# Re-laying a serial chain, its load queue and a job mixture in a fused attention and feed-forward backward kernel

## The chip, the cores and the metric

One core of one Trainium2 chip. The metric is the device time of one execution in microseconds (us). The kernel before takes 1837.25 us (median of 16 executions, 1830 to 1842).

## The reference, cut to what matters

The function is one decode step of a block with adaptive layernorm, and its backward pass: attention over a key and value cache of 2 x 32 heads x 8192 keys x 128, then a gated feed-forward layer. All gradients are outputs, those of both caches too.

```python
h = _layernorm(x) * (1 + ca) + sa
q = (h @ wq).reshape(B, 1, 32, 128).transpose(0, 2, 1, 3)
p = softmax(einsum('bhqd,bhkd->bhqk', q, k_cache) * 128 ** -0.5)
o = einsum('bhqk,bhkd->bhqd', p, v_cache)
x = x + ga * (o.reshape(B, 1, 4096) @ wo)
h = _layernorm(x) * (1 + cb) + sb
x = x + gb * ((silu(h @ w1) * (h @ w3)) @ w2)
# outputs: x, and the vjp for x, k_cache, v_cache, wq, wo, w1, w3, w2, c, w_mod
```

The caches are read (K once, V twice, because dV and dK need V again after the whole forward and feed-forward pass of that batch) and their gradients written. That is nearly all of the 718 MB that the kernel moves.

## The kernel before

The kernel is written as a static schedule. Work is put into numbered *slots*, and the slots are then emitted in order. A slot is a place in each engine's program, not a time. There are three kinds of work.

- An **A job** (64 of them, one for each batch and head, eight slots each): load K and V of the head, transpose K on TensorE, scores, exp, weighted sums of V and K.
- A **C job** (64, eight slots each): load V again, compute dV and dK on VectorE as outer products, store them. It needs dO of its head, so it can start only after its batch's chain.
- A **chain** for each batch: everything serial between that batch's last A job and its first C job, that is wo, layernorm, the feed-forward layer, its gradients and finally dO for all heads.

```python
def lay(steps, slot):                  # each step is (slots to advance, function)
    for n, f in steps:
        at(slot, PL_TASK, f)
        slot += n
    return slot

sA = [NG * i for i in range(H)]        # NG = 8: A jobs of batch 0
CS0 = end_a(sA[H - 1]) + 1             # 272: chain of batch 0 starts
TC = CS0 + length(ch[0]) + 1           # 330: chain (57 slots) is over
...
while len(sA) < NHD:                   # after TC, C and A jobs alternate
    if s >= TC and len(sC) < H and (not sC or sC[-1] < s - NG):
        sC.append(s)
    else:
        sA.append(s)
    s += NG
...
at(TC, PL_TASK, ffn_done)              # gives back two big buffers (w1, w3, w2)
```

The first C job comes at slot 336. Until then A jobs fill the slots, so the chain's instructions stand between theirs. The last part of the chain is dO: sixteen groups, each eight transposes of wo, one copy out of PSUM on VectorE, eight matmuls with one column, one group to a slot.

```python
def turned_steps(put, groups, done):
    ...
        nc.tensor.transpose(tp[:r, j, :], src, identb[:])
        kt = ktp.tile([P, GRP, P], BF16, name="kt", tag="kt")
        nc.vector.tensor_copy(kt[:r, 0:len(blocks), :], tp[:r, 0:len(blocks), :])
    ...
turned_steps(put, ogroups, lambda k, ps: nc.vector.tensor_copy(DO32[:, b, 2 * k:2 * k + 2], ps))
```

Loads are issued by one queue, in order of need. There are five *big* buffers (2 MB) and eleven *half* buffers (1 MB); V takes a big one, or two halves. The weights of the chain need big ones: two for wo, loaded once for both batches, and two for w1, w3 and w2, loaded again for batch 1.

```python
def pump():
    while loads:
        _, _, kind, f = loads[0]
        ...
        if kind == "big" and free["big"] < 1:
            return                     # nothing behind it is loaded either
        ...
        loads.pop(0)
        f()
```

## Time and profile before

| stretch of the span, us | what runs | GB/s | TensorE busy |
|---|---|---|---|
| 0 to 413 | A alone | 375 | 367 of 413 us |
| 413 to 497 | A and the chain of batch 0 | 293 | 74 of 84 us |
| 497 to 557 | A and dO of batch 0 | 285 | 55 of 60 us |
| 557 to 1128 | A and C in turn | 416 | 78% |
| 1128 to 1306 | C and the chain of batch 1 | 387 | 70% |
| 1306 to 1790 | C, small weight gradients | 416 | 71% |

The page shows the span in forty slices; each digit is a busy share in tenths, and the last line the rate of all DMA in each slice.

```profile
span 1835.9 us, 60759 instructions
...
PE   6988999898998777777778876677867777767561
...
DMA  9998998988679999999999999999999999999997
GB/s 386 421 411 323 377 399 327 418 316 332 252 288 373 425 417 421 420 423 419 417 421 407 416 423 393 414 356 377 422 408 412 412 416 424 418 423 402 427 418 292
```

From the thirteenth slice on the DMA engines are nearly always fully busy, at about 416 GB/s. There TensorE has room. In the slices just before, TensorE is at nine tenths and the rate falls to 252. So the kernel has two kinds of stretch, and time is to be had only where the rate is below 416. The windows view puts numbers on the stretches. Its columns are the window, its length, busy us of each engine with the count of instructions, the granted TensorE clock, the DMA engines' busy share, and GB/s.

```profile
core 0: us, PE busy (x) PEld busy (x) DVE busy (x) ACT busy (x) POOL busy (x), PEclk, DMA share, GB/s
0.00:413.00 413.00, 366.73 (x8603) 360.28 (x8604) 230.38 (x374) 225.70 (x305) 102.31 (x166) 0.99 0.95 375
413.00:497.00 84.00, 74.00 (x1693) 72.72 (x1690) 45.90 (x106) 34.98 (x49) 10.04 (x25) 0.88 0.77 293
497.00:557.00 60.00, 55.42 (x1283) 54.17 (x1280) 40.39 (x81) 26.93 (x39) 7.06 (x19) 0.97 0.76 285
557.00:1128.00 571.00, 444.49 (x8820) 430.69 (x8818) 386.51 (x456) 293.36 (x409) 99.15 (x205) 0.81 1.01 416
1128.00:1306.00 178.00, 125.42 (x2208) 116.98 (x2206) 135.82 (x223) 78.61 (x115) 21.93 (x41) 0.67 0.97 387
```

The view of waits, for the load queue on SyncE between 250 and 425 us, shows what held the loads (columns: who waited, for what, us in total, times, longest). L155 and L163 load K and V; L525 and L513 are loads of w1/w3 and of wo.

```profile
SPq L155 <- PE m_ps L455: 49.0, 12, 5.9
SPq L163 <- PE m_ps L455: 41.1, 8, 5.9
SPq L525 <- PE m_ps L455: 18.7, 2, 9.6
SPq L513 <- PE m_ps L455: 15.3, 2, 10.2
```

For 34 us the queue stood with a weight load at its head that waited for a big buffer. The Trainium skill ("DMA: Bandwidth & Descriptors", section "Anatomy of one DMA — SWDGE (gpsimd) path") says that a semaphore wait happens on the issuing sequencer before dispatch, not in the DMA engines. That section describes loads issued by GpSimd; these are issued by SyncE. The trace agrees: the wait stands on SyncE's sequencer, and no K or V load is issued behind it (none from 291.5 to 312 us, where the two buffers for w1, w3 and w2 are waited for).

### The profile page before, as it was taken

The numbers are of one execution on the slowest core, as the hardware profiler recorded it, in microseconds if no ns is written. First come the engines' busy times: TensorE is split into PE (matmuls) and PEld (weight loads), VectorE is DVE, ScalarE is ACT, GpSimd is POOL, SyncE is SP. The second block draws the span as 40 slices with busy tenths as digits, with TensorE's granted clock in tenths as the row PEclk, the third lists the DMA queues.
The fourth block names the chain that finished last, engine by engine and source line by source line (L and its number), as shares of the span: only waits on it lengthen the run. The fifth ranks groups of instructions, "written<-read, shape, count | busy, mean of one in ns | idle before, by whom it ended". The sixth has DMA issues, their size and how long they took to land. (4 is left out here: it accounts for less than half of the span.)

```text
span 1835.9 us, 60759 instructions
## 1 busy us (share of the span) xinstructions
PE 1416.7 (77%) x27206; PEld 1316.5 (72%) x27206; DVE 1177.8 (64%) x1602; ACT 953.9 (52%) x1359; POOL 330.8 (18%) x621
## 2 busy tenths in 40 slices
PE   6988999898998777777778876677867777767561
PEld 5988999898998777777778776676645555646561
DVE  2555556674666666667666667688845565656694
ACT  3555666554445455544555544434755565757451
POOL 0222222231012111111111111111111211111111
PEclk9999999998999788887887787577655555857675
DMA  9998998988679999999999999999999999999997
GB/s 386 421 411 323 377 399 327 418 316 332 252 288 373 425 417 421 420 423 419 417 421 407 416 423 393 414 356 377 422 408 412 412 416 424 418 423 402 427 418 292
DMA packets 99425, 718.11 MB, mean 391 GB/s; under 512 B 10160, under 2 KB 17020, under 8 KB 26332
## 3 DMA queue, kind: packets, MB, share of 16 engines
q1 hardware_dynamic: 57936, 430.00, 58.3%
q0 software_dynamic: 41216, 284.22, 37.3%
q8 instruction: 213, 3.49, 0.7%
q14 instruction: 48, 0.39, 0.1%
q10 hardware_dynamic: 12, 0.01, 0.0%
HBM read 429.99 MB, written 284.20 MB: 389 GB/s over the span
## 5 line engine op out<-in xcount | busy, mean ns | idle before, releaser
L395 ACT COPY kt<-tp 128x1024 bf16<-128x1024 bf16 x768 | 774.1, 1015 | 645.0 <-PE tp L390 636.9
L390 PE MATMUL tp<-identb,half 128*128 128x128 bf16 x5248 | 467.4, 241 | 38.9 <-issue 16.9
L455 PE MATMUL m_ps<-e,half 128*128 128x1 bf16 x4096 | 405.4, 170 | 3.1 <-issue 3.0
L390 PEld LDWEIGHTS <-half 128*128 128x128 bf16 x5248 | 355.4, 108 | 66.8 <-issue 43.4
L992 DVE TENSOR_TENSOR half<-DOr,e 128x2048 bf16<-128x2048 bf16 x256 | 311.8, 1218 | 131.4 <-DMA out_dram<-half 131.2
L992 DVE TENSOR_TENSOR half<-Qr,ds 128x2048 bf16<-128x2048 bf16 x256 | 310.2, 1220 | 78.7 <-DMA out_dram<-half 77.3
L455 PEld LDWEIGHTS <-half 128*128 128x128 bf16 x4096 | 353.3, 97 | 4.1 <-issue 3.9
L393 DVE COPY kt<-tp 128x1024 bf16<-128x1024 bf16 x256 | 176.2, 688 | 262.5 <-PE tp L390 251.7
L390 PE MATMUL tp<-identb,big 128*128 128x128 bf16 x2944 | 305.8, 267 | 13.3 <-DMA big<-in_A_v_cache_dram 12.3
L438 DVE TENSOR_TENSOR ek<-half,e 128x2048 bf16<-128x2048 bf16 x256 | 307.9, 1219 | 3.1 <-ACT e L430 2.2
L997 POOL DMA_DIRECT2D out_dram<-half x256 | 136.3, 532 | 954.0 <-DVE half L992 672.7
L390 PEld LDWEIGHTS <-big 128*128 128x128 bf16 x2944 | 230.8, 120 | 102.6 <-issue 88.8
L453 PE MATMUL m_ps<-ek,half 128*128 128x129 bf16 x2240 | 247.5, 228 | 55.8 <-DVE ek L438 54.8
L453 PEld LDWEIGHTS <-half 128*128 128x128 bf16 x2240 | 210.9, 106 | 60.0 <-issue 58.9
L969 PEld LDWEIGHTS <-kt 128*128 128x128 bf16 x4096 | 187.4, 108 | 80.6 <-DVE kt L393 51.7
L969 PE MATMUL s_ps<-DO_bf,kt 128*128 128x1 bf16 x4096 | 192.7, 168 | 67.9 <-DVE kt L393 47.1
L440 POOL COPY ek<-e 128x16 bf16<-128x16 bf16 x256 | 133.0, 540 | 431.8 <-ACT e L430 225.8
L411 PE MATMUL s_ps<-qT_bf,kt 128*128 128x1 bf16 x4096 | 178.5, 164 | 20.9 <-issue 9.5
L453 PE MATMUL m_ps<-ek,big 128*128 128x129 bf16 x1856 | 186.2, 218 | 3.9 <-issue 3.9
L411 PEld LDWEIGHTS <-kt 128*128 128x128 bf16 x4096 | 159.3, 97 | 26.2 <-issue 12.9
L453 PEld LDWEIGHTS <-big 128*128 128x128 bf16 x1856 | 156.9, 96 | 3.2 <-issue 3.0
L1113 ACT CAST stg<-m_ps 128x512 bf16<-128x512 f32 (+2 forms) x123 | 71.9, 594 | 113.4 <-DMA out_dram<-stg 96.2
(221 smaller groups left out, 805.4 us busy)
## 6 DMA issues: line engine op xcount, KB each, us to landing
out_dram<-half POOLq DMA_DIRECT2D x256, 1024.0 KB, 16.5
big<-in_A_v_cache_dram SPq DMA_DIRECT2D x75, 2048.0 KB, 17.3
half<-in_A_k_cache_dram SPq DMA_DIRECT2D x128, 1024.0 KB, 13.0
half<-in_A_v_cache_dram SPq DMA_DIRECT2D x106, 1024.0 KB, 21.1
out_dram<-stg POOLq DMA_DIRECT2D x22, 512.0 KB, 20.8
big<-in_B_w_dram SPq DMA_DIRECT2D x4, 1376.0 KB, 13.7
big<-in_A_wq_dram SPq DMA_DIRECT2D x8, 512.0 KB, 13.0
big<-in_A_wo_dram SPq DMA_DIRECT2D x2, 2048.0 KB, 9.5
```

The lines of the kernel that those rows point to most:

```text
L390: nc.tensor.transpose(tp[:, j, :], block(j), identb[:])
L393: nc.vector.tensor_copy(kt[:], tp[:])
L395: nc.scalar.copy(kt[:], tp[:])
L411: nc.tensor.matmul(S_ps[i][:, cc:cc + 1], kt[:, j, :], qT_bf[:, h, b:b + 1], start=True, stop=True)
L438: nc.vector.tensor_tensor(pair(t[:, :, 0:P]), pair(K[(i, hf)][:, o:o + QK, :]), E2[i][:, ks, :].unsqueeze(2).to_broadcast((P, QK, P // 2, ...
L440: nc.gpsimd.tensor_copy(t[:, :, P:P + 1], E2[i][:, ks, 0:1])
L453: nc.tensor.matmul(m[:, 0:P + 1], vb_(V[i], kk), t[:, kk % QK, 0:P + 1], start=(kk == 0), stop=(kk == KK - 1), skip_group_check=True)
L455: nc.tensor.matmul(m[:, P + 1:P + 2], kb_(K, i, kk), E2[i][:, kk, 0:1], start=False, stop=(kk == KK - 1), skip_group_check=True)
L969: nc.tensor.matmul(DP[n][:, cc:cc + 1], kt[:, j, :], DO_bf[:, b, h:h + 1], start=True, stop=True)
L992: nc.vector.tensor_tensor(pair(t[:, o:o + QK, :]), QD[(n, which)][:].rearrange("p (a b) -> p a b", b=2).unsqueeze(1).to_broadcast((P, QK, ...
L997: sq_.dma_start(src_of(dst, n)[:, hf * HK:(hf + 1) * HK, :], t[:])
L1113: nc.scalar.copy(st["t"][:lw, o:o + rw], ps[:lw, 0:rw])
```

## The change

The intent is to shorten the time in which TensorE works through A jobs and the chain together, and to start the C jobs, and with them the full DMA rate, earlier. It has five parts:

1. The chain is packed into 23 slots, several steps to a slot, and its dO part is taken out as separate steps. Batch 0's dO steps are strewn through the mixture of A and C, each just before the C jobs that need it.
2. The first C job comes at slot 304 instead of 336; A and C then alternate with 25 C jobs instead of 22.
3. The two feed-forward buffers are given back at slot 295 instead of 330.
4. A load that lacks a big buffer may be passed by the loads behind it (until slot 292).
5. dO's copies out of PSUM go from VectorE to ScalarE, and the layernorms' Sqrt and reciprocal become Ln and Exp.

```diff
-        nc.scalar.activation(std[:], s2[:], ACT.Sqrt, bias=eps_t[:], scale=1.0 / D)
-        nc.vector.reciprocal(rstd_t[:], std[:])
+        nc.scalar.activation(std[:], s2[:], ACT.Ln, bias=eps_t[:], scale=1.0 / D)
+        nc.scalar.activation(rstd_t[:], std[:], ACT.Exp, scale=-0.5)
 ...
     def pump():
-        while loads:
-            _, _, kind, f = loads[0]
+        j = 0
+        while j < len(loads):
+            _, _, kind, f = loads[j]
 ...
             if kind == "big" and free["big"] < 1:
-                return
+                if now[0] > CS0 + 20:
+                    return
+                j += 1
+                continue
 ...
-            loads.pop(0)
+            loads.pop(j)
 ...
+    def steps_do(b, k):                          # dO of two heads: tr, mm, sig
+        def tr():
+            ... eight transposes of wo into tp ...
+            nc.scalar.copy(kt[:], tp[:])
+        def mm():
+            ... eight matmuls with d_attn ...
+            nc.vector.tensor_copy(DO_bf[:, b, hs], ps)
+            nc.vector.tensor_mul(DOr_bf[:, b, hs], ps, rtot[:, b, hs])
+            ...
+        return [(1, tr), (1, mm), (1, sig)]
 ...
-        put(1, tot)
+        put(0, tot)                              # and so on for the other steps
 ...
-    TC = CS0 + length(ch[0]) + 1
+    E0 = CS0 + length(ch[0])
+    TC = E0 + 5
 ...
+    for k in range(H // 2):
+        lay(steps_do(0, k), E0 if k == 0 else max(E0 + 3 * k, sC[2 * k] - 10))
     t1 = lay(ch[1], CS1)
-    s = max(s, t1 + 4)
+    s = max(s, t1 + 5)
+    for k in range(H // 2):
+        lay(steps_do(1, k), t1)
+        t1 += 2
 ...
-    at(TC, PL_TASK, ffn_done)
+    at(E0, PL_TASK, ffn_done)
```

(The new loop that places the mixture, the changes of the other chain steps, and the removal of the old dO code are cut.)

More of the change, by code (lines that the diff above doesn't have):

```diff
@@ L544 @@
     O_bf = hcol("O_bf", BF16)
-    DO32 = hcol("DO32")
     DO_bf = hcol("DO_bf", BF16)
@@ L646, in tr, with sig @@
             st[("t", k)] = kt
-        def mm(k):
-            st[("p", k)] = groups[k][1](st.pop(("t", k)))
         def step(k):
-            if 0 <= k - 2 < len(groups):
-                done(k - 2, st.pop(("p", k - 2)))
             if k < len(groups):
                 tr(k)
-            if 0 <= k - 1 < len(groups):
-                mm(k - 1)
-        for k in range(len(groups) + 2):
+            if k > 0:
+                done(k - 1, groups[k - 1][1](st.pop(("t", k - 1))))
+        for k in range(len(groups) + 1):
             put(1, lambda k=k: step(k))
+    def steps_do(b, k):
+        out = []
+        st = {}
+        hs = slice(2 * k, 2 * k + 2)
+        def tr():
+            tp = tps.tile([P, GRP, P], BF16, name="tp", tag="tp")
+            for n in range(2):
+                for dc in range(NC):
+                    h = 2 * k + n
+                    nc.tensor.transpose(tp[:, n * NC + dc, :],
+                                        wo_v[h // (H // 2)][:, h % (H // 2), dc * P:(dc + 1) * P], identb[:])
+            kt = ktp.tile([P, GRP, P], BF16, name="kt", tag="kt")
+            nc.scalar.copy(kt[:], tp[:])
+            st["kt"] = kt
+        def mm():
+            ps = scr(2)
+            kt = st.pop("kt")
+            for n in range(2):
+                for dc in range(NC):
+                    nc.tensor.matmul(ps[:, n:n + 1], kt[:, n * NC + dc, :], d_attn_bf[:, dc, b:b + 1],
+                                     start=(dc == 0), stop=(dc == NC - 1))
+            nc.vector.tensor_copy(DO_bf[:, b, hs], ps)
+            nc.vector.tensor_mul(DOr_bf[:, b, hs], ps, rtot[:, b, hs])
+            pr = tmp.tile([P, 2], F32, name="prod", tag="prod", bufs=2)
+            nc.vector.tensor_mul(pr[:], O32[:, b, hs], ps)
+            st["pr"] = pr
+        def sig():
+            ps = scr(2)
+            nc.tensor.matmul(ps, onesf[:], st.pop("pr")[:], start=True, stop=True)
+            nc.vector.tensor_copy(SIG[:, b, hs], ps)
+        return [(1, tr), (1, mm), (1, sig)]
     def steps_chain(b):
@@ L679, in otask @@
             nc.vector.tensor_copy(O_bf[:, b, :], O32[:, b, :])
-        put(1, tot)
+            nc.vector.scalar_tensor_tensor(Qr_bf[:, b, :], qT[:, :, b], SCL, rtot[:, b, :], ALU.mult, ALU.mult)
+        put(0, tot)
         put(1, otask)
@@ L691, in attn_ev @@
             nc.vector.tensor_copy(attn[:, dc, b:b + 1], hold[dc])
-        for dc in range(NC):
-            def f(dc=dc):
-                if dc > 0:
-                    attn_ev(dc - 1)
-                attn_pe(dc)
-            put(1, f)
-        put(1, lambda: attn_ev(NC - 1))
+        put(1, lambda: (attn_pe(0), attn_pe(1)))
+        put(0, lambda: (attn_pe(2), attn_pe(3)))
+        put(0, lambda: [attn_ev(dc) for dc in range(NC)])
         def x1_task():
@@ L721, in ln_a @@
             nc.vector.tensor_sub(v[:], st[:, 1:2], sq[:])
-            hold["v"] = v
             hold["st"] = st
-        def ln_s():
-            nc.scalar.activation(hold["v"][:], hold["v"][:], ACT.Sqrt, bias=eps_t[:])
+            nc.scalar.activation(v[:], v[:], ACT.Ln, bias=eps_t[:])
+            nc.scalar.activation(rstd2[:, 0, b:b + 1], v[:], ACT.Exp, scale=-0.5)
         def ln_b():
-            nc.vector.reciprocal(rstd2[:, 0, b:b + 1], hold["v"][:])
             nc.vector.tensor_scalar(xn2[:, :, b], x1[:, :, b], hold["st"][:, 0:1], rstd2[:, 0, b:b + 1],
@@ L737, in steps_chain @@
         put(1, x1_task)
-        put(1, sums)
+        put(0, sums)
         put(1, ln_a)
-        put(2, ln_s)
         put(1, ln_b)
@@ L754, in proj_ev, with p1, p2 @@
             nc.vector.tensor_copy(dst[:FL, FC - 1, b:b + 1], hold[nm][:FL, FC - 1:FC])
-        put(1, lambda: proj("w1"))
-        def p2():
+        def p1():
+            proj("w1")
             proj_ev("w1", gate)
-            proj("w3")
-        put(1, p2)
-        def p3():
             hold["e"] = small(FC, "sge", b)
             nc.scalar.activation(hold["e"][:], gate[:, :, b], ACT.Exp, scale=-1.0)
+        put(1, p1)
+        def p2():
+            proj("w3")
             proj_ev("w3", up)
-        put(1, p3)
+        put(0, p2)
         def p4():
@@ L791, in p5 @@
             nc.vector.tensor_add(dslg[:, :, b], e[:], hold["sig"][:])
-        put(1, p5)
+        put(0, p5)
         def p6():
@@ L841, in q3 @@
             nc.vector.tensor_mul(d_attn_bf[:, :, b], mod[:, 2 * NC:3 * NC, b], d_x1[:, :, b])
-        put(1, q1)
-        put(1, sums)
+        put(0, q1)
+        put(1, lambda: None)
+        put(0, sums)
         put(1, q3)
-        ogroups = []
-        for h0 in range(0, H, 2):
-            def blocks(h0=h0):
-                return [wo_v[h // (H // 2)][:, h % (H // 2), dc * P:(dc + 1) * P]
-                        for h in (h0, h0 + 1) for dc in range(NC)]
-            def mm(kt):
-                ps = scr(2)
-                for n in range(2):
-                    for dc in range(NC):
-                        nc.tensor.matmul(ps[:, n:n + 1], kt[:, n * NC + dc, :], d_attn_bf[:, dc, b:b + 1],
-                                         start=(dc == 0), stop=(dc == NC - 1))
-                return ps
-            ogroups.append((blocks, mm))
-        turned_steps(put, ogroups, lambda k, ps: nc.vector.tensor_copy(DO32[:, b, 2 * k:2 * k + 2], ps))
-        def z1():
-            nc.vector.tensor_copy(DO_bf[:, b, :], DO32[:, b, :])
-            nc.vector.tensor_mul(DOr_bf[:, b, :], DO32[:, b, :], rtot[:, b, :])
-            nc.vector.scalar_tensor_tensor(Qr_bf[:, b, :], qT[:, :, b], SCL, rtot[:, b, :], ALU.mult, ALU.mult)
-            pr = small(H, "prod", b)
-            nc.vector.tensor_mul(pr[:], O32[:, b, :], DO32[:, b, :])
-            hold["pr"] = pr
-        def z2():
-            hold["sg"] = scr(H)
-            nc.tensor.matmul(hold["sg"], onesf[:], hold["pr"][:], start=True, stop=True)
-        put(1, z1)
-        put(1, z2)
-        put(1, lambda: nc.vector.tensor_copy(SIG[:, b, :], hold["sg"]))
         return out
@@ L900 @@
     s = NG * H
-    while len(sA) < NHD:
-        if s >= TC and len(sC) < H and (not sC or sC[-1] < s - NG):
+    while len(sA) < NHD and s < TC:
+        sA.append(s)
+        s += NG
+    na, ncc = NHD - len(sA), max(0, H - 1 - -(-(length(ch[1]) + 5 + MOFF) // NG))
+    for k in range(na + ncc):
+        if len(sC) * (na + ncc) <= k * ncc and len(sC) < ncc:
             sC.append(s)
@@ L913 @@
     lay(ch[0], CS0)
+    for k in range(H // 2):
+        lay(steps_do(0, k), E0 if k == 0 else max(E0 + 3 * k, sC[2 * k] - 10))
     t1 = lay(ch[1], CS1)
-    s = max(s, t1 + 4)
+    s = max(s, t1 + 5)
+    for k in range(H // 2):
+        lay(steps_do(1, k), t1)
+        t1 += 2
+    t1 += 1
     sC += [s + NG * n for n in range(H)]
```

## The prediction

> **What bounds the kernel now.** Bytes: the page shows 718 MB in 1836 us, 391 GB/s on average; stretches with fully busy DMA engines move about 416. By stretches: 0 to 413 us (phase A alone: transposed K, scores, exp, weighted sums) 375 GB/s, TensorE busy 367 us, near its limit; 413 to 497 us 293 GB/s and 497 to 557 us 285 GB/s, TensorE busy 74 of 84 and 55 of 60 us: here batch 0's serial chain (wo, layernorm, feed-forward and its gradients, dO) is interleaved with phase A; 557 to 1128 us, A and C (dV, dK) jobs alternating, 416 GB/s, TensorE 78% busy: DMA-bound; 1128 to 1306 us, batch 1's chain among C jobs, 387; C alone to 1790 us, 416; the tail 291. Time is to be had only where the rate is below 416.
>
> **What the change does.** It shortens the chain from 57 slots to 23 plus sixteen dO steps laid separately. Batch 0's dO steps are strewn, just in time, through the A/C mixture instead of preceding it; the first C job comes at slot 304 instead of 336, the mixture holds 25 C jobs instead of 22. No byte and hardly a matmul is removed. dO's sixteen 128x1024 copies per batch go from VectorE (0.69 us each) to ScalarE (1.01 us): 11 us of VectorE time per chain. Two feed-forward buffers come free 35 slots earlier. The load queue may pass a load that lacks a big buffer. Sqrt plus reciprocal become Ln and Exp: the trace has seven table loads of 1283 ns (the Trainium skill, "ScalarE: Activation LUTs", "What ACT_TABLE_LOAD costs", states the same number); at most a few us, mostly hidden.
>
> **What it is worth.**
> 1. Slots 272 to 304 hold the same TensorE work before and after (four A jobs, about 430 chain matmuls at 42 to 50 ns), so 413 to 497 us hardly moves. Fewer slots between dependent steps may cost TensorE 2 to 6 us; an earlier V load may give 4 us back.
> 2. The 60 us at 285 GB/s go into the DMA-bound mixture; dO's 256 matmuls (11 us) hide in 22% idle TensorE. Of 718 MB, 539 are still to move at 497 us: 1295 us at 416 GB/s, plus 14 us lost in the tail and 4 to 8 us in chain 1: about 1811. This step gains 60 x (1 - 285/416) = 19 us.
> 3. Chain 1: 178 us at 387 GB/s lose 12 us against 416. With 11 us less VectorE work (VectorE was 76% busy) half comes back: 6 us.
> 4. Prefetch and tables: 0 to 5 us.
> Sum about 28 us off 1837.
>
> **Predicted: 1808 us**, range 1788 to 1830. Chances: faster by over 2% 0.33, within 2% 0.63, slower 0.04.
>
> **What would show each step right.** 416 GB/s should be reached near 500 us instead of 560 to 600; the stretch before should look unchanged. The chain-1 stretch should run near 400 GB/s. Bytes, matmuls and the last slice should be the same; VectorE's busy time about 20 us lower, ScalarE's 30 us higher. Table loads should be fewer than seven.
>
> **What would make it wrong.** If the early mixture does not reach 416 GB/s, because the first C jobs' V loads come too late or buffers run short, step 2 shrinks. If the denser chain makes TensorE wait for VectorE and ScalarE, step 1 becomes a loss. If chain 1's stretch was limited by the weights' reload and held buffers rather than VectorE, step 3 is nothing; if VectorE was all of it, the gain doubles and 2% is passed. If the early feed-forward buffers lift the rate before 500 us too, it is faster still.

## The result, and the profile after

The changed kernel takes 1808.36 us (median of eight, 1803.63 to 1811.9). The ratio to the kernel before is 0.9842, with a 95% interval of 0.9826 to 0.9858: a gain of 1.6%, clear of noise but less than 2%.

The page after, same lines as above:

```profile
span 1801.9 us, 60973 instructions
...
PE   6888999999888887877877788788778684866761
...
DMA  9998999997899999999999999999999999999997
GB/s 385 421 422 346 388 385 388 361 376 282 324 384 422 410 421 420 413 416 414 419 414 409 417 415 419 400 412 386 402 417 415 413 412 426 419 422 418 410 423 294
```

The windows view of the changed kernel:

```profile
0.00:413.00 413.00, 368.63 (x8717) 362.62 (x8718) 233.58 (x376) 228.64 (x311) 101.93 (x170) 1.00 0.97 386
413.00:497.00 84.00, 75.08 (x1763) 73.17 (x1761) 52.84 (x123) 38.00 (x55) 12.61 (x28) 0.92 0.76 294
497.00:557.00 60.00, 50.81 (x1125) 48.58 (x1124) 42.13 (x55) 35.68 (x50) 13.54 (x24) 0.94 1.00 399
557.00:1128.00 571.00, 458.35 (x8925) 444.19 (x8923) 385.02 (x495) 301.61 (x417) 90.67 (x199) 0.80 1.01 416
1128.00:1306.00 178.00, 140.72 (x2411) 132.88 (x2409) 132.96 (x263) 97.54 (x136) 25.23 (x45) 0.68 1.00 400
```

The stretch from 413 to 497 us is as it was (294 GB/s against 293). From 497 to 557 us the rate is 399 instead of 285, and TensorE has room there. Two gains stand elsewhere: 386 instead of 375 GB/s before 413 us, and 400 instead of 387 in batch 1's chain. The mixture's rate did not change; it is the same 416.

The waits of the load queue, 250 to 425 us, in the changed kernel (L529 and L517 are the weights):

```profile
SPq L155 <- PE m_ps L459: 56.3, 13, 7.1
SPq L163 <- PE m_ps L459: 43.0, 8, 6.6
...
SPq L529 <- PE m_ps L459: 10.7, 2, 5.8
SPq L517 <- PE m_ps L459: 10.4, 2, 5.3
```

The weights now hold the queue for 21 us instead of 34. The queue doesn't wait less in all: with every row of the view added up it is 149 us, against 146 before. What changed is which loads stand behind a wait.

A rate in a fixed window mixes a gain with a shift. Since both kernels move the same 718 MB, a better measure is the time at which the first N megabytes had been started. I worked it out from the DMA packets' start times and sizes in the traces of one execution each:

```
first N MB    before    after    lead
    100        259.1    254.6     4.5
    160        424.9    414.3    10.6
    200        567.4    538.1    29.3
    440       1143.0   1114.9    28.1
    540       1395.2   1361.5    33.6
    700       1778.4   1745.1    33.3
```

The lead is made in three places: about 10 us before the chain of batch 0 has done anything (160 MB; the 4.5 us at 100 MB are within what two executions can differ by, see below), about 19 us between 160 and 200 MB, where the old kernel worked through dO, and about 5 us between 440 and 540 MB, where batch 1's chain lies. Elsewhere the two run alike. Traces of two executions can differ by several us without a reason: kernels that start with the same program as the kernel before differ from it by up to 3 us at 100 MB and 4.7 us at 80 MB. The profiled execution of the changed kernel was also its fastest (1803.63 us), so the 34 us between the two profiled spans stand for 29 in the medians.

### The profile page after: what moved, and what is told of

Same layout as the page of the kernel before. It is cut to its first block, busy times and chain, and to the rows that moved or that the text cites. A ratio compares the mean times of both kernels' runs of the same rounds, so it can differ in the third digit from the quotient of the medians.

```text
span 1801.9 us, 60973 instructions
## 1 busy us (share of the span) xinstructions
PE 1428.4 (79%) x27266; PEld 1326.8 (74%) x27266; DVE 1164.3 (65%) x1655; ACT 983.4 (55%) x1394; POOL 329.5 (18%) x621
## 5 line engine op out<-in xcount | busy, mean ns | idle before, releaser
L394 PEld LDWEIGHTS <-half 128*128 128x128 bf16 x5248 | 356.7, 108 | 48.5 <-issue 38.0
L459 PEld LDWEIGHTS <-half 128*128 128x128 bf16 x4096 | 352.7, 97 | 6.8 <-issue 6.6
L394 PEld LDWEIGHTS <-big 128*128 128x128 bf16 x2944 | 231.1, 120 | 111.7 <-issue 110.8
L457 PE MATMUL m_ps<-ek,half 128*128 128x129 bf16 x2112 | 234.7, 229 | 24.4 <-DVE ek L442 22.9
L457 PEld LDWEIGHTS <-half 128*128 128x128 bf16 x2112 | 200.0, 106 | 24.8 <-issue 24.6
L457 PE MATMUL m_ps<-ek,big 128*128 128x129 bf16 x1984 | 198.3, 217 | 3.4 <-issue 3.4
L444 POOL COPY ek<-e 128x16 bf16<-128x16 bf16 x256 | 125.7, 510 | 395.6 <-ACT e L434 189.7
L457 PEld LDWEIGHTS <-big 128*128 128x128 bf16 x1984 | 166.7, 96 | 2.0 <-issue 1.9
```

The source lines that it names most:

```text
L394: nc.tensor.transpose(tp[:, j, :], block(j), identb[:])
L444: nc.gpsimd.tensor_copy(t[:, :, P:P + 1], E2[i][:, ks, 0:1])
L457: nc.tensor.matmul(m[:, 0:P + 1], vb_(V[i], kk), t[:, kk % QK, 0:P + 1], start=(kk == 0), stop=(kk == KK - 1), skip_group_check=True)
L459: nc.tensor.matmul(m[:, P + 1:P + 2], kb_(K, i, kk), E2[i][:, kk, 0:1], start=False, stop=(kk == KK - 1), skip_group_check=True)
```

## The experiments

Theory P (the prediction): TensorE limits the stretch before the mixture and DMA limits the mixture, so what counts is that dO and four A jobs were moved from the one into the other. Rival S: the gain comes from what surrounds it, that is the shorter chain, earlier buffers, the load queue, or the other engine for the copies. The experiments ran in three batches, each on one chip with its own runs of the kernel before: first do_first, the two do_twice and do_copies_vector; then old_queue, sqrt_back, late_buffers and before_early_buffers; then the other four. The ratio to those runs is given for each. The changed kernel's own ratio (0.9842) comes from none of these batches, so a difference between two such ratios is certain to about 0.002 or 0.003 only, that is 4 to 5 us. Each batch holds one kernel that can't be told from the changed one: do_copies_vector (0.9839), sqrt_back (0.9861) and early_buffers_1 (0.9837). Against these the differences within a batch can be read too. Every kernel gave a correct result.

### do_first: the placement alone is undone

```diff
-    TC = E0 + 5
+    TC = E0 + 35
...
-        lay(steps_do(0, k), E0 if k == 0 else max(E0 + 3 * k, sC[2 * k] - 10))
+        lay(steps_do(0, k), E0 + 2 * k)
```

> The changed kernel with its short chain, its ScalarE copies and its early buffers, but batch 0's dO steps laid at two slots each before the mixture, and the first C job at slot 336 as in the kernel before (22 C jobs in the mixture's equal part). Theory P (placement: dO's matmuls and four A jobs were moved out of a TensorE-limited stretch into a DMA-bound one): most of the gain goes, about 1825 us (ratio to before 0.990 to 0.998). Rival S (the shorter chain, the freed buffers, the load queue or the move to ScalarE give the gain): stays at 1808 to 1813 us (ratio 0.984 to 0.987).

Measured: 1820.1 us, ratio 0.9911 (0.9898 to 0.9925). The placement is worth 0.9911 - 0.9842 = 0.0069 of 1837, 12.7 us (13 us against do_copies_vector of the same batch). The rest, 16 us, stays without it. So both theories hold a part. The windows view of this kernel shows the placement's part:

```profile
497.00:557.00 60.00, 58.42 (x1379) 57.79 (x1376) 39.65 (x84) 39.32 (x53) 12.98 (x24) 1.00 0.75 285
557.00:1128.00 571.00, 426.73 (x8525) 414.81 (x8522) 381.16 (x446) 289.21 (x404) 97.67 (x198) 0.80 1.00 416
```

TensorE is busy 58.4 of 60 us and the rate is 285 GB/s again, as before the change, although this kernel has the packed chain, the early buffers, the new queue and the copies on ScalarE. By the bytes moved, its lead over the kernel before is 13.3 us at 160 MB and 12.7 at 200, where the changed kernel goes from 10.6 to 29.3. So these four do not fill this stretch here while dO stands in it. (Early buffers alone, in the kernel before, do lift it in part; see before_early_buffers.)

### do_twice_before and do_twice_after: dO's TensorE work doubled

Every transpose and matmul of dO is done twice, with the same result. In the changed kernel:

```diff
-                for dc in range(NC):
+                for dc in [d for d in range(NC) for _ in range(2)]:
                     h = 2 * k + n
                     nc.tensor.transpose(...)
...
-            for n in range(2):
+            for n in (0, 0, 1, 1):
                 for dc in range(NC):
                     nc.tensor.matmul(...)
```

and the same doubling in the kernel before.

> The kernel before with every dO transpose and matmul done twice (256 matmuls more per batch, same result). Theory P: batch 0's 256 fall in a stretch where TensorE is the limit, about 42 ns each, so +8 to +14 us (1845 to 1851 us); batch 1's are mostly hidden. Rival (TensorE is not what holds that stretch, but buffers or waits): +0 to +4 us.

> The changed kernel with every dO transpose and matmul done twice. Theory P: hidden in the DMA-bound mixture, +0 to +3 us against the changed kernel (1808 to 1812 us, ratio to before 0.984 to 0.986). Rival (dO's TensorE time counts wherever it lies): +8 to +20 us (1816 to 1828 us).

Measured: before 1846.38 us, ratio 1.0056 (1.0040 to 1.0071), that is 10.3 us more, as theory P had it. The changed kernel: 1812.75 us, ratio 0.9878 (0.9861 to 0.9894), that is 6.6 us more than its own 0.9842: more than either 0 to 3 (theory P) or less than 8 to 20 (the rival). The traces show where. The windows view, kernel before with dO doubled:

```profile
497.00:557.00 60.00, 58.34 (x1409) 57.67 (x1406) 37.74 (x79) 23.05 (x32) 6.04 (x18) 1.00 0.66 243
```

and the changed kernel with dO doubled:

```profile
497.00:557.00 60.00, 53.42 (x1230) 51.70 (x1227) 46.35 (x60) 37.65 (x52) 17.02 (x29) 0.97 1.00 409
1128.00:1306.00 178.00, 146.40 (x2584) 140.61 (x2584) 127.02 (x260) 88.99 (x122) 23.17 (x41) 0.70 0.97 383
```

In the kernel before, doubling takes batch 0's stretch from 285 to 243 GB/s. In the changed kernel that stretch holds its rate (409): batch 0's dO is hidden in the mixture, as predicted. But batch 1's stretch falls from 400 to 383. By the bytes moved, it takes 253.6 us from 440 to 540 MB instead of 246.6. Batch 1's dO steps are packed one group to two slots among C jobs and are not hidden there. I had not thought of that half. Why they are not hidden is not shown: in the kernel before they stand still closer, one group to a slot, and doubling them cost that stretch nothing (252.2 us from 440 to 540 MB became 252.4).

### do_copies_vector: dO's copies on VectorE again

```diff
-            nc.scalar.copy(kt[:], tp[:])
+            nc.vector.tensor_copy(kt[:], tp[:])
             st["kt"] = kt
```

> The changed kernel with dO's copies out of PSUM on VectorE again. My step 3 (VectorE was half of what limited batch 1's chain stretch): +4 to +8 us, 1812 to 1817 us, all of it lost in that stretch, about 1130 to 1300 us into the span. Rival (that stretch is limited by the reload of the weights and the buffers they hold): within 2 us of 1808.

Measured: 1805.06 us, ratio 0.9839 (0.9822 to 0.9856): no difference. The windows view of this kernel:

```profile
1128.00:1306.00 178.00, 137.85 (x2425) 130.61 (x2422) 143.76 (x282) 80.40 (x119) 25.29 (x45) 0.69 1.00 401
```

VectorE works 11 us more in the stretch than in the changed kernel (143.8 against 133.0), and the rate is the same, 401. By the bytes moved, 440 to 540 MB take 246.4 us against 246.6. So taking the copies off VectorE is not what gave the gain in batch 1's chain. My step 3 named the wrong cause. (The reverse, moving only the copies in the kernel before, was not run.)

### old_queue and new_queue_alone: the load queue

The changed kernel with the old rule, and the kernel before with only the new one:

```diff
             if kind == "big" and free["big"] < 1:
-                if now[0] > CS0 + 20:
-                    return
-                j += 1
-                continue
+                return
```

(new_queue_alone is the reverse of this, put into the kernel before.)

> The changed kernel with the load queue of before, in which a load that lacks a big buffer stops all behind it. By the bytes moved against time the changed kernels are 8 to 12 us ahead of the kernel before already at 160 MB, before any chain step or C job is reached. Theory Q (the queue): this lead goes, and the total becomes 1815 to 1820 us (ratio to before 0.988 to 0.991), with the loads of the weights waiting 34 us at the queue's head again instead of 21. Rival (the lead is noise between executions or comes from Ln and Exp): within 3 us of 1808.

> The kernel before with only the new rule of the load queue. If the queue's worth is its own (the changed kernel with the old queue took 1814 us, about 6 more), it takes about 6 us off here too: 1829 to 1833 us (ratio 0.995 to 0.998), gained between 100 and 160 MB. If it only serves the early mixture: no difference, 0.998 to 1.002.

Measured: old_queue 1814.16 us, ratio 0.9883 (0.9862 to 0.9904), a loss of 7.5 us against 0.9842, but of only 4 us against sqrt_back of the same batch. new_queue_alone 1828.79 us, ratio 0.9958 (0.9938 to 0.9978), a gain of 7.7 us (4 to 11). So the rule is worth some us whether taken away or added alone; that it is worth the same in both kernels agrees with this, but is not shown so finely. In the traces the weights stand at the queue's head for 33 us in old_queue and 20 in new_queue_alone. The windows view shows what follows. The first window holds the wait for w1, w3 and w2, the second that for wo; the kernel before:

```profile
290.00:340.00 50.00, 47.66 (x1154) 47.18 (x1151) 29.60 (x43) 30.26 (x42) 13.27 (x22) 1.00 0.88 340
375.00:425.00 50.00, 42.98 (x1017) 42.10 (x1014) 33.50 (x59) 26.24 (x39) 15.38 (x20) 0.97 0.88 337
```

and new_queue_alone:

```profile
290.00:340.00 50.00, 47.36 (x1144) 46.92 (x1142) 29.34 (x41) 29.55 (x42) 11.30 (x22) 1.00 0.99 375
375.00:425.00 50.00, 44.73 (x1072) 43.99 (x1069) 34.51 (x64) 27.50 (x39) 15.49 (x20) 1.00 0.98 373
```

TensorE is nearly as busy, and the DMA engines move 375 and 373 GB/s instead of 340 and 337. All four kernels with the old rule lie at 330 to 341 in these windows, all ten with the new one at 359 to 387. The difference of some 3.5 MB is 8 us at 416 GB/s, an estimate from these lines. The lead at 160 MB follows the rule too, as far as single traces show it: 3.8 us with the old rule (1.4 in a second execution), 4.9 us with the new rule alone, 7.4 to 13.3 us in the changed kernel and the eight others made from it with the new rule.

### sqrt_back: Sqrt and reciprocal again

The edit puts back the two lines for Sqrt and reciprocal in both layernorms.

> The changed kernel with Sqrt and a VectorE reciprocal instead of Ln and Exp. The trace shows seven table loads of 1283 ns in both kernels, so nothing was saved there: expected within 3 us of 1808 (ratio 0.983 to 0.986). Rival (the table switch inside the chain is on TensorE's way): 4 us or more either way.

Measured: 1809.45 us, ratio 0.9861 (0.9838 to 0.9884). The difference of 3.5 us to 0.9842 is within the certainty of the comparison. A small gain by Ln and Exp is neither shown nor excluded. (If there is none, the whole batch reads 3.5 us too slow, and old_queue and late_buffers lose only 4 us each.) The number of table loads did not fall. Groups of the kernel before (line, engine, operation, count, busy us and mean ns, idle before):

```profile
L430 ACT ACT_TABLE_LOAD x2 | 2.6, 1283 | 0.0
L726 ACT ACT_TABLE_LOAD x2 | 2.6, 1283 | 0.0
L271 ACT ACT_TABLE_LOAD x1 | 1.3, 1283 | 1.9 <-issue 1.9
L247 ACT ACT_TABLE_LOAD x1 | 1.3, 1283 | 0.0
L766 ACT ACT_TABLE_LOAD x1 | 1.3, 1283 | 0.0
```

and of the changed kernel:

```profile
L756 ACT ACT_TABLE_LOAD x2 | 2.6, 1283 | 0.0
L757 ACT ACT_TABLE_LOAD x2 | 2.6, 1283 | 0.0
L271 ACT ACT_TABLE_LOAD x1 | 1.3, 1283 | 1.9 <-issue 1.9
L247 ACT ACT_TABLE_LOAD x1 | 1.3, 1283 | 0.0
L248 ACT ACT_TABLE_LOAD x1 | 1.3, 1283 | 0.0
```

L756 and L247 are the Ln, L757 and L248 the Exp that follows it. Each of the three Ln and each of the three Exp got a load of its own, so there are seven loads in both kernels. The Trainium skill ("ScalarE: Activation LUTs", section "Table sets: the hidden batching unit") says that Ln followed by Exp needs one load, because one set has both. This program did not get it so; the measurement decides. The trace doesn't say which set was loaded.

### late_buffers and before_early_buffers: when the feed-forward buffers come free

```diff
-    at(E0, PL_TASK, ffn_done)
+    at(E0 + 35, PL_TASK, ffn_done)        # late_buffers, in the changed kernel
...
-    at(TC, PL_TASK, ffn_done)
+    at(CS0 + 34, PL_TASK, ffn_done)       # before_early_buffers, in the kernel before
```

> The changed kernel with the two feed-forward buffers given back at slot 330, as before, instead of 295. Theory P with buffers as a condition: V of the jobs at slots 296 to 320 is loaded only when halves come free, TensorE waits for it, and 8 to 16 us of the gain between 180 and 200 MB go (1816 to 1824 us). Rival (buffers don't matter, placement alone does): within 3 us of 1808.

> The kernel before with only this changed: the two feed-forward buffers are given back when their last reader is done (slot 306) instead of slot 330. Theory P: that stretch is TensorE-limited, so at most 4 us are gained (1832 to 1836 us). Rival S (buffers starve the loads there and cost the time): 10 us or more, 1826 us or less.

Measured: late_buffers 1815.35 us, ratio 0.9884 (0.9863 to 0.9905), a loss of 7.7 us (4 us against sqrt_back of the same batch), under the 8 to 16 us that were expected. before_early_buffers 1833.67 us, ratio 0.9980 (0.9957 to 1.0002), a gain of 3.7 us, with an interval from none to 8. Yet its trace shows that early buffers can lift the stretch while dO stands in it, from 285 to 341 GB/s with TensorE just as busy:

```profile
497.00:557.00 60.00, 56.28 (x1344) 55.16 (x1340) 43.71 (x83) 28.73 (x44) 8.94 (x22) 1.00 0.87 341
```

Its lead over the kernel before grows from 1.7 us at 180 MB to 11.4 at 200, and is 6.5 at 440. So in this one trace the stretch's rate depends on the buffers that loads can run ahead into too, not on TensorE alone. The windows view of late_buffers, followed by the same windows of the changed kernel:

```profile
413.00:453.00 40.00, 37.65 (x783) 37.35 (x784) 19.22 (x58) 14.27 (x21) 2.23 (x8) 0.66 0.60 223
453.00:493.00 40.00, 36.75 (x863) 35.61 (x861) 26.62 (x57) 19.86 (x28) 5.20 (x14) 1.00 0.70 252
```

```profile
413.00:453.00 40.00, 36.56 (x859) 35.84 (x857) 21.52 (x65) 16.14 (x23) 3.00 (x11) 0.83 0.64 244
453.00:493.00 40.00, 36.17 (x854) 35.15 (x851) 28.13 (x55) 21.22 (x31) 8.18 (x14) 1.00 0.88 341
```

Between 453 and 493 us TensorE does the same work in both (36.8 and 36.2 us busy, 863 and 854 matmuls), but the loads run at 252 instead of 341 GB/s. I had expected TensorE to wait for V; from 425 to 560 us it does so for 2.6 us only. What is lost is loading ahead: late_buffers is 2.7 us behind the kernel before at 180 MB, where the changed kernel is 13.2 us ahead. My reading is that a byte that could have moved while TensorE was the limit has to be moved later, when DMA is. (In the first of the two windows the granted clock was also lower, 0.66 against 0.83, in these two executions; how much of the 7.7 us that is stays open.)

### long_chain_1: batch 1's chain, one step to a slot

```diff
     ch = [steps_chain(b) for b in range(B)]
+    ch[1] = [(max(1, n), f) for n, f in ch[1]]
```

(and the mixture's count is computed with the length of batch 0's chain, so that it stays the same)

> The changed kernel with batch 1's chain laid one step to a slot (31 slots instead of 23), all else the same. The changed kernels, with dO copies on either engine, lose about 6 us less than the kernel before between 440 and 540 MB. Theory L (the chain's length there does it): 2 to 6 us are lost again, 1810 to 1814 us. Rival (the place of the chain and of the weights' reload among the C jobs does it): within 2 us of 1808.

Measured: 1813.79 us, ratio 0.9873 (0.9853 to 0.9894), 5.7 us more than 0.9842 (6.6 us more than early_buffers_1 of the same batch), as theory L expected. But the trace does not show the loss in that stretch. The time from 440 to 540 MB, one execution of each kernel:

```
old chain, old place:      before 252.2   do_twice_before 252.4   new_queue_alone 252.7   before_early_buffers 253.4
packed chain, new place:   after 246.6    do_first 246.7   do_copies_vector 246.4   sqrt_back 247.0   old_queue 247.3
packed chain, new place:   late_buffers 249.2
others:                    long_chain_1 249.5   do_twice_after 253.6
                           early_buffers_1 243.1   early_buffers_1_slow_do 240.1
```

Within each of the first two rows the kernels lie within 1.2 us, but late_buffers, whose chain of batch 1 is the same as in the second row, is 2.4 us above that row's mean. So a difference of 2 to 3 us between single traces can't be read for certain here. The change gained 5.9 us in this stretch (means 252.7 and 246.8, or 5.5 with late_buffers), which can. Of long_chain_1's loss the trace puts 2.7 us into the stretch, no more than late_buffers has there without a longer chain. It was behind at 440 MB already (a lead of 22.2 us instead of 28.1), before batch 1's chain has done much, where the program is that of the changed kernel; that part is difference between executions. So the runs say that the longer chain costs time, and the traces do not show that it costs it here. What gives the 5.9 us is open.

### early_buffers_1 and early_buffers_1_slow_do: further in the same direction

The experiments pointed to two things left in batch 1: its feed-forward buffers are still held through dO, and its dO steps are not hidden.

```diff
+    E1 = t1
     for k in range(H // 2):
         lay(steps_do(1, k), t1)
-        t1 += 2
+        t1 += 3                            # only in early_buffers_1_slow_do
...
     at(E0, PL_TASK, ffn_done)
+    at(E1, PL_TASK, ffn_done)
...
     def chain_done():
-        wn.clear()
         wo_v.clear()
-        release("big", 4)
+        release("big", 2)
```

> The changed kernel with batch 1's feed-forward buffers given back before its dO steps, not after them, as batch 0's already are. Late buffers cost 7 us in batch 0; here V loads in slots 751 to 784 get two big buffers more. If that stretch is short of buffers: 3 to 8 us faster, 1800 to 1805 us (ratio 0.980 to 0.983). If not: within 2 us of 1808.

> The kernel early_buffers_1 with batch 1's dO steps laid every three slots, not every two. Doubling dO's TensorE work cost the changed kernel some 10 us between 480 and 520 MB, where batch 1's dO steps lie, so they are not hidden there: if thinner dO steps hide better, 1 to 5 us under early_buffers_1; if the stretch is bound by something else, no difference.

Measured: 1806.68 us, ratio 0.9837 (0.9816 to 0.9858), and 1804.81 us, ratio 0.9825 (0.9805 to 0.9845). Neither can be told from the changed kernel's 0.9842. In the stretch itself both work: 3.5 and 6.5 us less from 440 to 540 MB (table above), and the windows view of early_buffers_1_slow_do shows nearly the full rate:

```profile
1128.00:1306.00 178.00, 133.65 (x2277) 127.26 (x2276) 135.90 (x262) 89.44 (x121) 25.24 (x45) 0.66 1.01 414
```

By the end most of it is given back: its lead over the kernel before is 37.4 us at 540 MB and 32.2 us at 700 MB, where the changed kernel goes from 33.6 to 33.3. Both kernels beat the kernel before; that either beats the changed one is not shown, and where the rest went stays open.

## Why the prediction was right, point by point

1808 us were predicted, 1808.36 measured. The main mechanism is shown. That the total is right to 1 us is luck: step 2 was too large, step 4 too small, the cause in step 3 was wrong, and these made up for each other.

1. *Step 1, the stretch from 413 to 497 us hardly moves*: right. 294 GB/s against 293, TensorE 75.1 us busy against 74.0. From the exp of A job 32 to that of job 37, 85.7 us became 82.1 (84.7 to 86.1 in three other kernels with the same program there). The packed chain did not make TensorE wait noticeably longer.
2. *Step 2, dO and four A jobs go into the mixture, 19 us*: the mechanism is right and was shown by undoing it (285 GB/s comes back) and by doubling dO (285 falls to 243 before, hidden after). The size was somewhat high: 12.7 us when it alone is undone. It also rests on the early buffers, without which 4 to 7.7 us of the gain go. It needs the packed chain of batch 0 too, without which C could not start at slot 304; no run undoes that packing.
3. *Step 3, batch 1's chain, 6 us by relief of VectorE*: the size is right (5.9 us from 440 to 540 MB), the cause wrong. With the copies back on VectorE the time and the rate are the same. Undoing the packing of this chain costs 5.7 us in all, but the traces do not show it in this stretch; what gave the 5.9 us is open.
4. *Step 4, prefetch and tables, 0 to 5 us*: probably under-sized. The queue alone is worth 4 to 8 us. The tables gave nothing that could be measured, and the forecast of fewer than seven loads was wrong: there are seven.

The parts, 12.7 + 5.9 + 4 to 7.5 for the queue + 0 to 3.5 for Ln and Exp, come to 23 to 30 us; the medians differ by 29. This is no independent check: the 5.9 is read from traces, and what late_buffers and long_chain_1 lose (7.7 and 5.7 us) belongs in part to the same terms, since losses by undoing one part at a time need not add up. Of the other signs, the bytes are the same, the last slice is as slow (294 against 292 GB/s), ScalarE's busy time rose by 29.5 us (30 were forecast) and VectorE's fell by 13.5 (20 were forecast).

What brought the total near is the way in which step 2 was computed: not from the work removed, for there was none, but from the bytes still to move at the point where the DMA-bound stretch begins, and the rate measured there. With what the changed kernel's trace shows, 534 MB still to move at 497 us instead of 539, 399 GB/s until 557 us instead of 416, and 7 and 13 us lost in batch 1's chain and the tail, the same sum gives 1803 us, and the profiled execution took 1803.6.

## What to carry to other kernels

In a kernel that alternates between stretches bound by compute and by DMA, no work need be removed to save time: moving compute from the first into the idle engine time of the second can save what the DMA engines would have missed. The length of the stretch times the missing share of the rate gives an upper estimate (19 us here, of which 12.7 were measured). In a compute-bound stretch a byte loaded ahead can be time saved later, so a buffer given back sooner, or a queue that doesn't stop behind one load, can count there even when hardly any engine is seen waiting for data. And that an engine is busy does not show that it bounds a stretch; moving work off it or doubling it does: VectorE was 76% busy in batch 1's chain, and in the changed kernel 11 us more of its work there changed nothing.

## What the Trainium skill lacked or had wrong

- "ScalarE: Activation LUTs", section "Table sets: the hidden batching unit": Ln then Exp is said to cost one table load, since one set has both. Here each Ln and the Exp after it had a load each, seven loads of 1283 ns in all, as many as with Sqrt.
- Not a fault, but confirmed: the same page's 1283 ns for one table load (section "What ACT_TABLE_LOAD costs") is exactly what all fourteen loads of the two traces show.
- "DMA: Bandwidth & Descriptors", section "Where 436 GB/s comes from", says that for transfers between HBM and SBUF the HBM side at about 358 GB/s binds. With one core at work, this kernel held 416 GB/s of mixed reads and writes for 571 us. The sentence needs "with both cores of a pair at work": the page's own table of measured rates has 425 GB/s for one core alone, and 416 agrees with that.
- No page that I read says what a load at a queue's head that waits for a buffer costs the kernel: here letting others pass it raised the rate around the waits from 340 and 337 GB/s to 375 and 373, and was worth 4 to 8 us.
